# A gated feature map in two passes: 16 rows of pass two loaded between the passes instead of 16 kept rows at the end of pass one

## The chip, the cores and the metric

The kernel runs on one core of a Trainium2 chip. The metric is the device time of one execution in microseconds; the median of three runs of the kernel before is 722.75 us (721.04 to 722.99).

## The reference

```python
x: (1, 384, 384, 384) bf16, w1d: (1,) bf16
g = jnp.einsum("bhwc->bc", x) / (H * W)      # mean of each channel
s = sigmoid(g * w1d[0])                      # k = 1: one weight
return x * s[:, None, None, :]               # every pixel scaled per channel
```

The scale of each channel needs all of x, and each value of x is needed again once the scale is known. x has 113 MB, as has the result.

## The kernel before, in words

**Layout.** The 147456 pixels are 1152 "rows" on 128 partitions: a row holds one pixel of 384 channels on each partition, 768 bytes per partition and 98,304 bytes in all. SBUF holds an arena of 275 rows (line 188). The program gives it names by row number: U = 108, G0 = 116, V = 212, A = 220, T = 259, Y = 267.

**Pass one** reads all 1152 rows. SyncE issues the loads (`load`, line 231); TensorE adds each row to one accumulator in PSUM with a matmul against ones (`sum_rows`, line 253, recorded at line 242). Some of the rows are *streamed*: read, summed, overwritten. The others are *kept*, so that pass two needn't read them again. Two kinds are kept:
- Folded groups. The bf16 values of x are small enough that the upper exponent bits are known; `fold` (line 292, VectorE lines 276 and 282, ScalarE's test line 313) stores the bits of every fourth row in those spare bits of three others, so 32 rows (16 or 24 in two of the groups) take three quarters of their place. It works in a scratch of 16 rows, T and Y. Group 1 lies at rows 12 to 43, group 2 at 116 to 147, and so on in two columns.
- Raw rows, N_RAW of them: U (8 rows), V (8), the three slots of 13 rows from A on, and before the change also Y (8) and T (8), loaded when the last group is folded and the scratch is free (lines 437 and 438).

What is neither is streamed: N_STREAM = 1152 - N_RAW - 296, here 785. The order of pass one's loads is written out: group 9 (24 rows), group 0 (16 rows), then the head of the stream (lines 402 to 412), then each of the groups 1 to 8 followed by the streamed rows that `BETWEEN` gives it (361 rows in all), then the raw rows. The head has `first` = N_STREAM - 361 = 424 rows: first the remainder by 48 (40 rows) into rows 172 to 211, then loads of 48 rows that go round the slots 28 to 75, 76 to 123, 124 to 171 and 172 to 219, eight of them. Group 1 comes next, then 48 rows into 68 to 115.

**Order and waits.** `Flow` (line 21) records every instruction with the arena rows that it reads and writes and puts in the semaphore waits: a load waits until the instructions that last used its rows are done. All loads and stores of both passes go through SyncE's queue (L236 loads, L466 stores) in the order in which they were recorded; an instruction that waits holds up those behind it.

**The scale.** After the last sum ScalarE computes `s_bf` (line 443) and copies it to PSUM (line 447). VectorE then multiplies (`scale`, line 451), and SyncE stores.

**Pass two.** A planner in the program (lines 564 to 760) orders VectorE's and SyncE's work by its own costs per row: scaled pieces are stored, groups are unfolded (`unfold`, line 470) when the rows that they need for scratch are stored (`needed`, line 607), and streamed rows are loaded again into rows that have become free. `landed` is its list of pieces that are ready to scale; before, it starts with Y, U, T, V and two of the slots (lines 620 to 623). `todo` counts the streamed rows that were given out for loading.

Of the kernel before, what the change touches and what calls it, by code (L numbers as in the profile page):

```python
# [127 lines left out]
def kernel(  # L128
# [26 lines left out]
    PAIR = 2 * PIECE  # L155
    PAIRS = 4
    U = 3 * PIECE + PAIRS * 3 * PAIR
    G0 = U + PAIR
    V = G0 + PAIRS * 3 * PAIR
    A = V + PAIR  # L160
    N_A = 39
    T = A + N_A
    Y = T + 2 * PIECE
    ROWS = Y + 2 * PIECE
# [9 lines left out]
    BANKED = len(GROUPS)  # L174
    GROUPS.append((A, 6))
    PS = 3 * GROUPS[BANKED][1]
    N_RAW = ROWS - V + PAIR
    pool = ctx.enter_context(tc.tile_pool(name="sb", bufs=1))
    psum = ctx.enter_context(tc.tile_pool(name="psum", bufs=1, space=bass.MemoryType.PSUM))

# [21 lines left out]
    def view(t, r0, n):  # L202
        return t[r0 * P : (r0 + n) * P, :].rearrange("(p r) c -> p r c", r=n)

    def rows(lo, n):
        return [("a", r) for r in range(lo, lo + n)]
# [4 lines left out]

    N_STREAM = RPP - N_RAW - sum(4 * q for _, q in GROUPS)
    N_KEPT = RPP - N_STREAM
    assert N_STREAM % 2 and N_KEPT % 2
    STREAMED, KEPT = (0, N_STREAM), (N_STREAM, N_KEPT)
# [5 lines left out]
    c_raw = r  # L221
    assert r + N_RAW == N_KEPT

    def raw(a):

        return c_raw + (a - U if a < G0 else PAIR + a - V)
# [4 lines left out]
    def load(chunk, a, lo, hi):  # L231

        r0, n = chunk
        fl.add(
            "SP",
            lambda: nc.sync.dma_start(out=arena[:, a : a + hi - lo, :], in_=view(xf, r0, n)[:, lo:hi, :]),  # L236
            writes=rows(a, hi - lo), dma=True,
        )
# [150 lines left out]
    for i, bk in enumerate(banks):  # L389
        lo, hi = i * BANK, min((i + 1) * BANK, PS * C)  # L390
# [3 lines left out]
    S1, S2, S3 = ([slot] for slot in SLOTS)  # L394
# [38 lines left out]
    def take_raw(a, n):  # L433
        load(KEPT, a, raw(a), raw(a) + n)
        sum_rows(a, n)

    for a, n in S2 + [(U, 8)] + S3 + S1 + [(V, 8), (Y, 8), (T, 5), (T + 5, 3)]:
        take_raw(a, n)
    assert summed[0] == RPP

    fl.add(
        "ACT",
# [128 lines left out]
    moves, waiting, over, acts = deque(), deque(), deque(), deque()  # L571
    landed = deque()
    idle = [False] * ROWS
    todo = 0

    def release(a, n):
        for i in range(a, a + n):
# [39 lines left out]
        return f  # L617


    for a, n, end in ((Y, 4, True), (Y + 4, 4, True), (U, 4, True), (U + 4, 4, True), (T, 8, True), (V, 8, True)):  # L620
        landed.append((KEPT, a, raw(a), n, end))
    for a, n in SLOTS[:2]:
        landed.append((KEPT, a, raw(a), n, True))

# [63 lines left out]
    while True:  # L688

        if dve_at <= now:  # L690
# [4 lines left out]
            if landed and (ahead < PENDING or not can):  # L695
                chunk, a, lo, n, end = landed.popleft()
# [13 lines left out]
        if alongside and alongside[0][0] <= now:  # L710
            _, chunk, a, lo, n = alongside.popleft()
            store(chunk, a, lo, lo + n)
            moves.append([now + LAT, n * ROW + PER_STORE, stored(a, n)])
        while waiting and waiting[0][0] <= now:
            _, n, then, chunk, a, lo, known = waiting.popleft()
# [12 lines left out]
        if bank_at is None and len(line) <= total - BANKS_AT and got and max(got)[0] >= PS * 4 // 3:  # L728
            a = max(got)[1]
# [3 lines left out]
            for i, bk in enumerate(banks):  # L733
                lo, hi = i * BANK, min((i + 1) * BANK, PS * C)
# [4 lines left out]
        if got and todo < N_STREAM:  # L739
            n, a = max(got)  # L740
            n = min(n, CAP, N_STREAM - todo)
# [52 lines left out]
```

## Time and profile before

| what | value |
|---|---|
| median of three runs | 722.75 us |
| profiled execution, first to last instruction (span) | 719.4 us |
| VectorE busy | 493.9 us (69%) |
| TensorE busy | 213.0 us (30%) |
| ScalarE busy | 115.7 us (16%) |
| bytes moved | 303.79 MB, 422 GB/s over the span |
| read from HBM, written to HBM | 190.41 MB, 113.25 MB |

The page gives busy time per engine, then the span in 40 slices of 18 us in tenths of busy time. PEclk is TensorE's granted clock. In answers with windows the columns after the length are busy time and number of instructions of TensorE, its weight loads, VectorE, ScalarE and GpSimd, then granted clock, the mean busy share of the 16 DMA engines, and GB/s. In a timeline a row is start, duration, engine, line, operation and count, and in brackets the engine's idle time before it and what ended it.

### The profile page before, as it was taken

How to read it: one execution, taken by the hardware profiler on the slowest of the kernel's cores; microseconds unless marked ns; L12 is line 12 of the kernel's file. 1: busy time of each engine (PE TensorE's matmuls, PEld its weight loads, DVE VectorE, ACT ScalarE, POOL GpSimd, SP SyncE). 2: the span in 40 equal slices, each digit the busy share in tenths (PEclk: the TensorE clock that was granted, in tenths of full speed). 3: DMA queues.
4: the chain of work that ended last, by engine and by line, in shares of the span. 5: the costliest groups of instructions: out<-in, count | busy, mean ns of one | idle time of the engine just before them, and what ended most of it. 6: DMA issues, size and time to landing. Idle time of an engine off the chain costs nothing.

```text
span 719.4 us, 2061 instructions
## 1 busy us (share of the span) xinstructions
PE 213.0 (30%) x1202; PEld 0.3 (0%) x3; DVE 493.9 (69%) x471; ACT 115.7 (16%) x93; POOL 10.6 (1%) x7
## 2 busy tenths in 40 slices
PE   4677788897987770000000000000000000000000
PEld 0000000000000000000000000000000000000000
DVE  4600004788999719988999998999998985095500
ACT  3600003566677610002000000000000000000000
POOL 0000000000000005000000000000000000000000
PEclk9899999999999995555555555555555555555555
DMA  9999999999999979999999999999999999999997
GB/s 379 435 433 435 426 428 435 438 434 425 426 426 429 427 326 376 421 391 423 430 430 437 430 428 441 428 433 435 430 436 433 429 437 428 441 432 427 440 439 314
DMA packets 20174, 303.79 MB, mean 422 GB/s; under 512 B 2243, under 2 KB 2243, under 8 KB 6083
## 3 DMA queue, kind: packets, MB, share of 16 engines
q1 hardware_dynamic: 20160, 303.67, 99.0%
q8 instruction: 4, 0.07, 0.0%
q14 instruction: 8, 0.06, 0.0%
q10 hardware_dynamic: 2, 0.00, 0.0%
HBM read 190.41 MB, written 113.25 MB: 422 GB/s over the span
## 4 chain that ended last, share of the span: by engine, by line
DMA 63%; DVE 23%; PE 6%; ACT 2%; another core or an unknown queue 1%; SPq 1%; issue 0%; DVEq 0%
DMA arena<-in_x_dram 42%; DMA out_dram<-arena 20%; DVE arena L456 16%; PE bank L242 6%; DVE arena L276 4%; DVE arena L282 3%; ACT arena L313 2%; SPq L236 1%; ACT s_bf L443 0%; SPq L789 0%; DVEq L112 0%; SPq L106 0%
## 5 line engine op out<-in xcount | busy, mean ns | idle before, releaser
L456 DVE TENSOR_TENSOR arena<-arena,s_bf 128x4608 bf16<-128x4608 bf16 (+8 forms) x97 | 228.7, 2390 | 68.2 <-DMA arena<-in_x_dram 52.2
L276 DVE TENSOR_SCALAR arena<-arena 128x1536 uint16<-128x1536 uint16 (+2 forms) x247 | 145.3, 633 | 111.6 <-DMA arena<-in_x_dram 101.8
L242 PE MATMUL bank<-arena,ones 128*128 128x384 bf16 x1151 | 204.6, 339 | 46.3 <-DMA arena<-in_x_dram 46.3
L313 ACT ACTIVATE arena<-arena 128x3072 uint16<-128x3072 uint16 (+1 forms) x38 | 102.4, 2696 | 142.1 <-DVE arena L276 142.1
L282 DVE TENSOR_TENSOR arena<-arena 128x1536 uint16<-128x1536 uint16 (+2 forms) x114 | 121.0, 1061 | 5.2 <-PE bank L242 2.8
L529 PE MATMUL bank<-odd,ones 128*128 128x1 bf16 x1 | 0.2, 187 | 322.6 <-DVE odd L524 322.6
L456 POOL TENSOR_TENSOR arena<-arena,s_bf 128x1536 bf16<-128x1536 bf16 (+1 forms) x3 | 10.4, 3481 | 268.7 <-ACT bank L447 268.7
L386 ACT COPY arena<-bank 128x512 uint32<-128x512 uint32 (+1 forms) x7 | 4.0, 570 | 58.2 <-DMA out_dram<-arena 58.1
L456 DVE TENSOR_TENSOR arena<-arena,bank 128x1536 bf16<-128x1536 bf16 (+2 forms) x7 | 11.3, 1689 | 0.0
L242 PE MATMUL bank<-zeros,ones 128*128 128x384 bf16 x48 | 8.3, 326 | 0.0
L313 ACT ACTIVATION_READ_ACCUMULATOR arena<-arena 128x1 f32 x38 | 7.1, 186 | 0.0
L386 ACT COPY bank<-arena 128x512 uint32<-128x512 uint32 (+1 forms) x7 | 3.6, 567 | 0.0
L443 ACT ACTIVATE s_bf<-bank,w_sc 128x384 bf16<-128x384 f32 x1 | 0.6, 580 | 14.5 <-PE bank L242 14.5
L256 PE MATMUL bank<-arena,ones 128*128 128x384 bf16 x1 | 0.5, 480 | 6.8 <-DMA arena<-in_x_dram 6.8
L762 ACT ACT_TABLE_LOAD x1 | 1.3, 1283 | 0.7 <-PEq L778 0.7
L343 DVE TENSOR_SCALAR w_sc<-bank 128x1 f32<-128x1 f32 x1 | 0.2, 157 | 1.2 <-PE bank L338 1.2
L333 DVE MEMSET ones<- 128x128 bf16 x1 | 0.2, 165 | 1.0 <-SPq L106 1.0
L338 PE MATMUL bank<-w_bf,ones 1*128 1x1 bf16 x1 | 0.2, 179 | 2.2 <-DMA w_bf<-in_w1d_dram 2.2
L529 PEld LDWEIGHTS bank<-odd,ones 128*128 128x128 bf16 x1 | 0.1, 105 | 581.5 <-DVE odd L524 581.5
L533 DVE CAST odd_i<-bank 128x1 int32<-128x1 f32 x1 | 0.2, 157 | 0.3 <-PE bank L529 0.3
L447 ACT COPY bank<-s_bf 128x192 uint32<-128x192 uint32 x1 | 0.3, 322 | 0.0
L519 DVE TENSOR_REDUCE worst<-seen 128x1 f32<-128x38 f32 x1 | 0.2, 186 | 0.0
(8 smaller groups left out, 0.9 us busy)
## 6 DMA issues: line engine op xcount, KB each, us to landing
arena<-in_x_dram SPq DMA_DIRECT2D x15, 4608.0 KB, 34.8
arena<-in_x_dram SPq DMA_DIRECT2D x21, 1248.0 KB, 13.5
out_dram<-arena SPq DMA_DIRECT2D x7, 3072.0 KB, 33.1
arena<-in_x_dram SPq DMA_DIRECT2D x6, 3072.0 KB, 27.5
out_dram<-arena SPq DMA_DIRECT2D x4, 4608.0 KB, 39.3
arena<-in_x_dram SPq DMA_DIRECT2D x6, 2304.0 KB, 18.5
arena<-in_x_dram SPq DMA_DIRECT2D x3, 4512.0 KB, 27.1
out_dram<-arena SPq DMA_DIRECT2D x10, 1248.0 KB, 11.9
```

The source lines that it names most:

```text
L236: lambda: nc.sync.dma_start(out=arena[:, a : a + hi - lo, :], in_=view(xf, r0, n)[:, lo:hi, :]),
L242: return pe.add_instruction(mybir.InstMatmult(name=nc.get_next_instruction_name(), ins=[pe.lower_ap(rhs), pe.lower_ap(ones[:])], outs=[pe. ...
L256: return nc.tensor.matmul(acc, lhsT=ones[:], rhs=arena[:, i, :], start=first, stop=last)
L276: lambda: nc.vector.tensor_scalar(out=dst, in0=src, scalar1=s0, scalar2=s1, op0=op0, op1=op1),
L282: "DVE", lambda: nc.vector.tensor_tensor(out=dst, in0=a, in1=b, op=op), reads=reads, writes=writes
L313: lambda: nc.scalar.activation(out=y, in_=y, func=ACTF.Copy, accum_out=seen[:, 2 * k + i : 2 * k + i + 1]),
L386: "ACT", lambda: nc.scalar.copy(dst.bitcast(u32), src.bitcast(u32)), reads=reads, writes=writes
L443: lambda: nc.scalar.activation(out=s_bf[:], in_=acc, func=ACTF.Sigmoid, scale=w_sc[:, 0:1]),
L447: "ACT", lambda: nc.scalar.copy(s_ps.bitcast(u32), s_bf[:].bitcast(u32)), reads=["s_bf"], writes=["bank0"]
L456: lambda: vec.tensor_tensor(out=v, in0=v, in1=s[:, None, :].to_broadcast([P, n, C]), op=Op.mult),
L529: lambda: nc.tensor.matmul(votes, lhsT=ones[:], rhs=odd[:], start=True, stop=True),
L762: nc.scalar.preload_act_table(ACTF.Sigmoid)
```

## The change

The rows Y and T are no longer kept. N_RAW falls from 71 to 55, and N_STREAM rises from 785 to 801, so that the head of pass one has 440 rows: 8, and nine loads of 48. The raw rows now end with V, cut into 5 and 3. Behind the last load of pass one, and ahead of the scale in the program, stand two loads of 8 rows each, the first 16 rows of the stream, into Y and T; they are not summed there, but in their turn at the head of pass one. The planner starts with `todo` = 16, and with U (2, 2 and 4 rows) and V (4 and 4) ahead of Y and T.

```diff
-    N_RAW = ROWS - V + PAIR
+    N_RAW = T - V + PAIR
+    N_AHEAD = ROWS - T
...
-    for a, n in S2 + [(U, 8)] + S3 + S1 + [(V, 8), (Y, 8), (T, 5), (T + 5, 3)]:
+    for a, n in S2 + [(U, 8)] + S3 + S1 + [(V, 5), (V + 5, 3)]:
         take_raw(a, n)
     assert summed[0] == RPP
+
+
+    for a, lo in ((Y, 0), (T, PAIR)):
+        load(STREAMED, a, lo, lo + PAIR)
+    assert N_AHEAD == 2 * PAIR
...
-    todo = 0
+    todo = N_AHEAD
...
-    for a, n, end in ((Y, 4, True), (Y + 4, 4, True), (U, 4, True), (U + 4, 4, True), (T, 8, True), (V, 8, True)):
-        landed.append((KEPT, a, raw(a), n, end))
+    for a, n in ((U, 2), (U + 2, 2), (U + 4, 4), (V, 4), (V + 4, 4)):
+        landed.append((KEPT, a, raw(a), n, True))
+    for a, lo in ((Y, 0), (T, PAIR)):
+        landed.append((STREAMED, a, lo, PAIR, True))
```

## The prediction

> **What bounds the kernel now.** I read the page first: the span, the 40 slices, then the chain of waits that ended last.
>
> ```profile
> span 719.4 us, 2061 instructions
> ...
> PE   4677788897987770000000000000000000000000
> ...
> DMA  9999999999999979999999999999999999999997
> GB/s 379 435 433 435 426 428 435 438 434 425 426 426 429 427 326 376 421 391 423 430 430 437 430 428 441 428 433 435 430 436 433 429 437 428 441 432 427 440 439 314
> ```
>
> The DMA row is 9 in all slices but the one where pass one turns into pass two and the last one. Moving bytes sets the time, in both passes; any time in which the DMA engines have nothing queued is added to the end. The span is 719.4 us and the median of the runs 722.75, so 3.4 us lie around it; I add my sum to both.
>
> Next, the hand-over between the passes, in windows of 2 us, and one window fitted to the hole.
>
> ```profile
> 264.00:266.00 2.00, 1.83 (x13) 0.00 (x0) 0.00 (x0) 0.00 (x0) 0.00 (x0) 1.00 0.75 302
> 266.00:268.00 2.00, 2.00 (x13) 0.00 (x0) 0.00 (x0) 0.00 (x0) 0.00 (x0) 1.00 0.09 36
> 268.00:270.00 2.00, 0.09 (x1) 0.00 (x0) 1.26 (x2) 0.90 (x2) 0.86 (x1) 1.00 0.00 0
> 270.00:272.00 2.00, 0.00 (x0) 0.00 (x0) 2.00 (x3) 0.00 (x0) 2.00 (x1) 1.00 0.73 295
> ...
> 266.84:270.58 3.74, 1.25 (x8) 0.00 (x0) 1.84 (x3) 0.90 (x2) 1.44 (x1) 1.00 0.00 0
> ```
>
> The last two columns are the DMA share and GB/s. Most engines run out near 265, the last one at 266.84, and nothing moves until 270.58: 3.74 us of idle on the last engine. That hole is what the change means to use.
>
> Then I asked in which order pass one's loads may be issued, for the change alters that list too: SyncE's waits, the chain inside pass one, and TensorE's timeline there.
>
> ```profile
> SPq L236 <- PE bank L242: 168.0, 23, 26.8
> ```
>
> ```profile
> 88.16 8.28 PE bank L242 x40
> 96.44 0.02 issue
> 96.45 31.90 DMA arena<-in_x_dram
> ```
>
> ```profile
> 43.61 9.64 PE L242 MATMUL bank<-arena,ones 128*128 128x384 bf16 x48 [2.91 <-DMA arena<-in_x_dram]
> 55.55 7.96 PE L242 MATMUL bank<-arena,ones 128*128 128x384 bf16 x48 [2.30 <-DMA arena<-in_x_dram]
> 66.42 9.64 PE L242 MATMUL bank<-arena,ones 128*128 128x384 bf16 x48 [2.91 <-DMA arena<-in_x_dram]
> 77.29 7.96 PE L242 MATMUL bank<-arena,ones 128*128 128x384 bf16 x48 [1.22 <-DMA arena<-in_x_dram]
> 88.16 9.56 PE L242 MATMUL bank<-arena,ones 128*128 128x384 bf16 x48 [2.91 <-DMA arena<-in_x_dram]
> ...
> 109.92 0.32 PE L242 MATMUL bank<-arena,ones 128*128 128x384 bf16 x1 [2.94 <-DMA arena<-in_x_dram]
> ```
>
> A load waits until TensorE has summed the rows that it overwrites (168 us of such waits), but each wait ends while two or three loads of 48 rows are still queued. The load issued at 96.45 takes 31.90 us to land: it stands in a long queue, and so the waits cost nothing.
>
> **Part 1: the hand-over, 16 rows more in a hole.** Pass one reads 1152 rows either way. Pass two reads 801 rows instead of 785, so 16 rows (128 x 16 x 768 bytes, 1.573 MB) are moved in addition; the window 112 to 262 ran at 429 GB/s, which makes 3.7 us. They go into the hole: Y and T are free once the folding is done, at 253.5 in the trace (ScalarE's last test ends at 253.45), long before the DMA queue reaches them, so the two loads follow pass one's last bytes without a gap and end where pass one's bytes end now, in the same place of the queue. What remains of the hole: TensorE's last rows are now V, not T. All in today's times: the row "261.59 3.57 x21" sums the slot before V and V and ends at 265.16; from the last sum to VectorE's first scale were 0.65 us (268.09 to 268.74); a scale of 2 rows I estimate at 0.5 from the rows of 4 (0.96) and 13 (2.76); from the store's issue to its first packet were 0.85 (269.73 to 270.58). The first store moves at 267.2, the last engine is free at 266.84: 0.4 us are left of 3.74. Saved 3.3; the 16 rows, which pass one now reads ahead of this point, push all of it back by 3.7: **+0.4 us**. The bounds are 0 (the sums keep up with the bytes) and +3.7 (the first stores come no earlier). Everything after that is the same work: 1152 rows stored, 785 loaded. One scale more on VectorE (about 0.1 us) lies beside the stores, which it feeds at 0.22 us a row against 0.23 us of DMA; without that cover it costs its 0.1.
>
> **Part 2: the order of pass one's loads, which the change shifts without saying so.** N_STREAM rises from 785 to 801. The loads that stand between the groups are fixed (361 rows), so the head of pass one gets 440 rows instead of 424: 8 + 9 x 48 instead of 40 + 8 x 48. The 48-row loads go round four slots (28 to 75, 76 to 123, 124 to 171, 172 to 219). Before, the eighth ends in the slot 172 to 219. After, the ninth goes to 28 to 75. The next load in SyncE's queue is group 1, rows 12 to 43, and it overlaps 28 to 43. Before, that slot was written four loads back: the group's load was issued at 80.08, after 16 matmuls of the batch that began at 77.29, with 144 rows (33 us) queued behind. After, it must wait until the load **just ahead of it** has landed and 16 of its rows are summed, with nothing queued behind. SyncE issues in order, so all later loads stand behind this wait. The DMA engines run dry, and pass one has no slack elsewhere to give it back.
>
> The price: from the last packet to the landing 0.28 (266.84 to the landing event at 267.12); from the landing to the issue 2.83 as the trace has it now (77.25 to 80.08, TensorE at granted clock 1.00), or more at half clock; then 0.85 to the first packet (1.01 for the kernel's first load, 0.96 to 1.97). At full clock that is 4.0. At half clock: from 88.12 to 92.5 TensorE did 17 matmuls at granted clock 0.62, and in the batch at 66.42 the sixteenth ended near 70.4; so 16 matmuls take 4.0 to 4.3 and the hole is 5.1 to 5.5. Which one? Four batches began after an idle time of 2.9 us, and three of them show half clock and 9.6 us; the slow batches come in turn with fast ones, and by that turn the ninth load falls on a slow one. I take 4.1: **0.28 + 4.1 + 0.85 = 5.2 us**. The mean engine ends 1.7 us before the last one (at 265 against 266.84 at the hand-over), so seen from it the hole is up to 7; both ends, 4.0 and 7, go into the range.
>
> [...]
>
> Is there a second hole? The load after group 1 (rows 68 to 115) waits for all 48 rows of the same ninth load: 8.0 to 9.7 us after its landing, plus 0.9; group 1's 32 rows keep the engines busy until 3.7 + 7.3 = 11.0 (full clock) or 5.0 + 7.3 = 12.3 (half). Covered by 1.3 us or more. The two loads behind that wait for nothing new, and from group 1's landing on, loads, sums and folding stand to each other as now: the queue is 112 to 128 rows deep again two loads later.
>
> **Part 3: pass two's plan.** The planner starts from other pieces and sends U and V first, Y and T last, and all later loads are cut anew. Reading SyncE's queue with the rows that stand behind each awaited store, the thinnest cover is 21 rows now and 21 after; at the end, the last load still has 36, 16, 16, 16 and 8 rows of stores behind it, and VectorE's 3.4 us for 16 rows stay under the DMA's 3.7. I cost this at nothing. The unknown: the front of pass two moves fewer bytes, with the engines counted busy:
>
> ```profile
> 272.00:290.00 18.00, 0.00 (x0) 0.00 (x0) 17.97 (x15) 0.00 (x0) 7.52 (x3) 0.51 1.02 396
> 290.00:320.00 30.00, 0.00 (x0) 0.00 (x0) 27.28 (x27) 0.00 (x0) 0.00 (x0) 0.50 1.00 402
> 320.00:700.00 380.00, 0.19 (x1) 0.10 (x1) 306.92 (x236) 3.99 (x7) 0.00 (x0) 0.50 1.01 433
> ```
>
> Against 433 the first two windows lose 1.5 and 2.1 us, together 3.7; most of it in 280 to 284 (326 GB/s) and 312 to 316 (274). Whether another order has this too, the trace can't say: between -3.7 and +3.7, taken at 0, since the pieces there stay as small.
>
> **Sum:** 0.4 + 5.2 + 0 = +5.6 us: span 725.0, time 722.75 + 5.6 = **728.3 us**. Its own range: 4.0 to 7 for the hole, 0 to 1 for the hand-over, 726.7 to 730.8.
>
> **Rivals.**
> - *The hole is short or partly paid back*: full clock (4.0), the sums keep up (0), part of the slow front doesn't return (up to -2.4): 724.3 to 726.7. For it: the batch at 109.92, after 2.94 us idle, ran at full speed. Chance 0.18.
> - *No hole*: the load of group 1 finds rows queued behind, as the waits of now do, and only the hand-over counts: 722.75 + 0.4 = 723.2. Against it: the row numbers above leave nothing behind it. Chance 0.05.
> - *Faster*: the order of pass two's front decides. Before, stores and loads alternate from 278.7 on; after, all kept rows are stored first and four loads follow in a row. If the alternation makes the slow front, it is won back: -3.7. It decides only where the hole is under 1.1 us (0.4 + 1.1 - 3.7 = -2.2); with no hole the time is 719.5. Against it: loads and stores alternate later too, at 433. Chance 0.03.
> - *The change doesn't do what it says*: the 16 rows are not hidden, since stores start no earlier than they would behind them or lose as much to them: +3.7 instead of +0.4, 731.6; with a long hole up to 733. Against it: 253.5 lies 13 us ahead of the hand-over. Chance 0.09.
>
> The forecast has 0.65. The range leaves out the two small cases, the lower end of the first rival and the upper end of the last: 725.2 to 731.2. Within 0.3% (720.6 to 724.9, about what a measurement of this kernel can tell from no change) fall the case without a hole and the lower end of the short one: 0.10. Faster 0.03, slower 0.87.
>
> **What would show it.** In the changed profile: a window of some 4 us near 110 to 120 with the DMA share near 0, with SyncE waiting for TensorE, and TensorE idle some 5 us more behind the ninth 48-row load (right: part 2; absent: wrong). No window of 2 us at 0 at the hand-over, and pass two's first store about 5.5 us later than 270.58 (part 1). From there to the end the same length within 2.5 us (part 3). A faster kernel, or a slower one without that hole, makes the prediction wrong.

## The result and the profile after

The changed kernel takes 730.31 us (median of 4 runs, 728.17 to 730.75) against 722.5 (721.04 to 722.99): ratio 1.0108, 95% interval 1.0096 to 1.0121, so 7.8 us slower. The profiled execution is the one of 728.17 us with a span of 726.4, so 1.8 us lie around its span; the span of 719.4 before then very likely belongs to the run of 721.04, with 1.6 us around it, and not to the median. Span against span the change costs 7.0 us.

The page of the changed kernel, the lines that answer to those of before:

```profile
span 726.4 us, 2070 instructions
...
PE   5686776988897771000000000000000000000000
...
DMA  9999996999999998999999999999999999999997
GB/s 378 434 421 449 428 424 286 434 433 434 422 425 427 428 426 366 389 428 428 427 426 429 436 424 442 425 431 436 433 434 441 433 423 446 427 428 442 424 431 320
```

The 7 at the hand-over (326 and 376 GB/s in two slices) has become an 8 (366 and 389). But the seventh slice, in the middle of pass one, has fallen from 435 to 286 GB/s. In windows of 2 us around it, with the DMA share and GB/s at the end of each line, and one window fitted to the silence:

```profile
108.00:110.00 2.00, 2.00 (x14) 0.00 (x0) 0.00 (x0) 0.00 (x0) 0.00 (x0) 1.00 0.80 340
110.00:112.00 2.00, 2.00 (x14) 0.00 (x0) 0.00 (x0) 0.00 (x0) 0.00 (x0) 1.00 0.74 313
112.00:114.00 2.00, 0.77 (x6) 0.00 (x0) 0.00 (x0) 0.00 (x0) 0.00 (x0) 1.00 0.05 18
114.00:116.00 2.00, 2.00 (x13) 0.00 (x0) 0.00 (x0) 0.00 (x0) 0.00 (x0) 1.00 0.00 0
116.00:118.00 2.00, 2.00 (x15) 0.00 (x0) 0.00 (x0) 0.00 (x0) 0.00 (x0) 1.00 0.54 135
118.00:120.00 2.00, 2.00 (x14) 0.00 (x0) 0.00 (x0) 0.00 (x0) 0.00 (x0) 1.00 0.66 270
...
113.55:117.67 4.12, 3.75 (x24) 0.00 (x0) 0.00 (x0) 0.00 (x0) 0.00 (x0) 1.00 0.00 0
```

The hole stands at its forecast place, with a slope on each side: the engines don't stop together (a share of 0.80, 0.74 and 0.05 from 108 to 114), and they don't start at full rate (270 GB/s in 118 to 120). TensorE and SyncE there, in two timelines of the changed kernel:

```profile
103.05 9.64 PE L243 MATMUL bank<-arena,ones 128*128 128x384 bf16 x48 [2.91 <-DMA arena<-in_x_dram]
113.92 7.96 PE L243 MATMUL bank<-arena,ones 128*128 128x384 bf16 x48 [1.23 <-DMA arena<-in_x_dram]
126.49 7.69 PE L243 MATMUL bank<-arena,ones 128*128 128x384 bf16 x32 [4.60 <-DMA arena<-in_x_dram]
```

```profile
116.71 0.33 SPq L237 DMA_DIRECT2D arena<-in_x_dram  x1
```

The ninth load lands at 113.88, its sums begin at 113.92, and the load of group 1 goes out at 116.71: 2.83 us after the landing, as it did before, but now with nothing queued behind it.

### The profile page after: what moved, and what is told of

It is laid out like the page before. It is cut to its first block, busy times and chain, and to the rows that moved or that the text cites. A ratio compares the mean times of both kernels' runs of the same rounds, so it can differ in the third digit from the quotient of the medians.

```text
span 726.4 us, 2070 instructions
## 1 busy us (share of the span) xinstructions
PE 213.4 (29%) x1202; PEld 0.3 (0%) x3; DVE 494.0 (68%) x473; ACT 115.7 (16%) x93; POOL 10.2 (1%) x7
## 4 chain that ended last, share of the span: by engine, by line
DMA 62%; DVE 22%; PE 8%; another core or an unknown queue 5%; ACT 1%; issue 0%; SPq 0%
DMA arena<-in_x_dram 48%; DVE arena L462 15%; DMA out_dram<-arena 14%; PE bank L243 8%; DVE arena L277 4%; DVE arena L283 3%; ACT arena L314 1%; SPq L237 0%; ACT s_bf L449 0%; SPq L472 0%; SPq L797 0%; SPq L112 0%; SPq L106 0%
## 5 line engine op out<-in xcount | busy, mean ns | idle before, releaser
L462 DVE TENSOR_TENSOR arena<-arena,s_bf 128x4608 bf16<-128x4608 bf16 (+9 forms) x98 | 228.4, 2363 | 91.6 <-DMA arena<-in_x_dram 78.6
L462 DVE TENSOR_TENSOR arena<-arena,bank 128x1536 bf16<-128x1536 bf16 (+3 forms) x8 | 11.8, 1544 | 0.0
```

The source lines that it names most:

```text
L462: lambda: vec.tensor_tensor(out=v, in0=v, in1=s[:, None, :].to_broadcast([P, n, C]), op=Op.mult),
```

## Where the 7 us are: lost bytes, stage by stage

The DMA engines move 433 GB/s in the middle of pass two of the kernel before (320 to 700; 431 in the changed one), and I take 433 as the full rate for both. So the time that a stretch loses is its length times (433 - its GB/s) / 433. Three stretches, before (first fence) and after (second), the later ones shifted with the first store:

```profile
90.00:150.00 60.00, 52.37 (x305) 0.00 (x0) 27.02 (x37) 20.05 (x15) 0.00 (x0) 0.96 1.00 433
...
258.00:274.00 16.00, 8.61 (x50) 0.00 (x0) 5.26 (x6) 0.90 (x2) 4.86 (x2) 0.95 0.70 288
274.00:326.00 52.00, 0.00 (x0) 0.00 (x0) 49.25 (x42) 0.00 (x0) 5.52 (x2) 0.50 1.01 402
```

```profile
90.00:150.00 60.00, 48.38 (x269) 0.00 (x0) 19.09 (x26) 14.28 (x10) 0.00 (x0) 0.91 0.91 388
...
265.00:281.00 16.00, 8.78 (x53) 0.00 (x0) 4.60 (x6) 0.90 (x2) 4.20 (x2) 0.91 0.87 359
281.00:333.00 52.00, 0.00 (x0) 0.00 (x0) 49.72 (x42) 0.00 (x0) 5.77 (x2) 0.50 1.01 413
```

| stretch | lost before | lost after | difference |
|---|---|---|---|
| ahead of group 1 (60 us) | 0.0 | 6.2 | +6.2 |
| hand-over (16 us) | 5.4 | 2.7 | -2.7 |
| 16 rows more, 1.573 MB at 433 GB/s | | 3.6 | +3.6 |
| front of pass two (52 us) | 3.7 | 2.4 | -1.3 |

The sum is +5.8 of the 7.0. The first row depends on the edges of its window by up to 1 us: 100 to 140, at 355 GB/s, gives 7.2. The landings of later loads need no window and give 6.6 (below the table of the four holes). What then remains, 0.8, is spread out, most of it over the long rest of pass two (431 GB/s from 333 to 720, 432 before from 326 to 713).

## The experiments

The theory on trial: the order of pass one's loads makes nearly all of the loss, and the change itself (16 rows more, hidden in the hand-over) is about even. The rivals: the additional rows and pass two's new plan cost; or pass one pays the hole back.

**1. The changed kernel with the slots turned,** so that the ninth load ends where the eighth did.

```diff
-    EARLY = [(A - 48 * i, 48) for i in (4, 3, 2, 1)]
+    EARLY = [(A - 48 * i, 48) for i in (1, 4, 3, 2)]
```

> The changed kernel, with one edit: the nine 48-row loads at the head of pass one start at the slot 172 to 219, so that the ninth ends there again, as the eighth did before, and the load of group 1 waits for rows that were loaded four loads back. Theory (the hole ahead of group 1 is nearly the whole cost): the hole is gone, DMA share 0.9 or more in all windows of 2 us from 100 to 130, and the time is that of the kernel before plus the 0.4 us of the hand-over: 722.5 to 723.5. Rival (the 16 additional rows and pass two's new order cost): it stays at 728 or more.

722.11 us against 721.89, ratio 1.0004 (0.9995 to 1.0013). Three windows of it, the last two for the hand-over and the front of pass two:

```profile
90.00:150.00 60.00, 49.76 (x292) 0.00 (x0) 24.82 (x34) 18.83 (x13) 0.00 (x0) 0.97 1.00 432
258.00:274.00 16.00, 9.23 (x55) 0.00 (x0) 4.16 (x6) 0.90 (x2) 3.76 (x2) 0.94 0.88 364
274.00:326.00 52.00, 0.00 (x0) 0.00 (x0) 49.93 (x42) 0.00 (x0) 6.21 (x2) 0.50 1.01 415
```

The hole is gone and with it the whole loss. What the change says of itself costs nothing that can be measured, and wins nothing. The expected share of 0.9 in every window of 2 us was asked too sharply: packets count where they start, so that such windows swing (0.77 in 100 to 102, 1.24 in the next), and the kernel before swings as much (0.68 in 124 to 126). The time lies below the expected 722.5 to 723.5 because the kernel before ran at 721.89 here, and not at 722.5.

**2. The hole alone, in the kernel before.** Nothing of the change is in it; the eight loads start one slot later.

```diff
-    EARLY = [(A - 48 * i, 48) for i in (4, 3, 2, 1)]
+    EARLY = [(A - 48 * i, 48) for i in (3, 2, 1, 4)]
```

> The kernel before, with one edit: the eight 48-row loads start one slot later, so that the eighth ends in 28 to 75 and group 1's load must wait for it; nothing of the change itself is in. Theory, by lost bytes (the windows 108 to 122 of the changed kernel move 3.06 MB less than at 434 GB/s, that is 7.0 us): 722.5 + 7.0 = 729.5. Second theory, by the last DMA engine's idle time alone (4.0 us between its packets): 726.5. Rival (the hole is paid back later in pass one, and pass two costs): 722.5.

729.12 against 721.89, ratio 1.0097 (1.0081 to 1.0112): +7.2 us, as the first theory has it (its 3.06 MB are 3.11 by the windows of 2 us of the trace, that is 7.2 us and not 7.0). Together with the first experiment this settles the cause from both sides. Here TensorE ran the sums that group 1's load waits for at half clock (the batch at 109.97 took 9.43 us, granted clock 0.50 up to 113, and the load went out at 114.22, 4.30 after the landing at 109.92). The hole is longer for it:

```profile
90.00:150.00 60.00, 50.52 (x274) 0.00 (x0) 21.13 (x29) 15.89 (x11) 0.00 (x0) 0.89 0.89 379
109.58:115.17 5.59, 5.20 (x24) 0.00 (x0) 0.00 (x0) 0.00 (x0) 0.00 (x0) 0.70 0.01 3
```

No data packet moves for 5.6 us (the 3 GB/s are one packet of the instruction queue, q8, at 111.03), but 60 x (433 - 379) / 433 = 7.5 us of bytes are lost.

**3. The ninth load in two pieces,** 20 and 28 rows in the same slot.

```diff
-    stream_all(EARLY, first - first % 48)
+    stream_all(EARLY, first - first % 48 - 48)
+    stream_all([(A - 192, 20), (A - 172, 28)])
```

> The changed kernel, with the ninth 48-row load cut into 20 rows (28 to 47) and 28 rows (48 to 75) in the same slot. Group 1's load still waits for the load just ahead to land and 16 of its rows to be summed, but 28 rows (6.4 us) are queued behind that. Theory (what costs is that nothing is queued, not the wait): no hole, since landing, sums and first packet take 4.0 us; 722.5 to 723.5, as with the slots turned. Rival (the wait itself, or the slot order, costs): 728 or more.

724.97, ratio 1.0048 (1.0034 to 1.0062): +3.1 us, a miss of the expectation, though far from the rival's 728. The timeline shows what the expectation left out:

```profile
103.22 15.96 PE L243 MATMUL bank<-arena,ones 128*128 128x384 bf16 x96 [2.92 <-DMA arena<-in_x_dram]
```

The piece of 20 rows lands at 107.73, but TensorE is still summing the load ahead of it and comes to these rows only near 111; group 1's load goes out at 113.81, when the 28 rows behind are all but read.

```profile
90.00:150.00 60.00, 50.60 (x292) 0.00 (x0) 22.06 (x30) 16.86 (x11) 0.00 (x0) 0.94 0.96 410
113.96:114.76 0.80, 0.76 (x5) 0.00 (x0) 0.00 (x0) 0.00 (x0) 0.00 (x0) 1.00 0.00 0
```

The miss teaches more than a hit would have: all engines are silent for 0.8 us only, yet 3.2 us of bytes are lost, and the time is 3.1 longer. The silence of the last engine is not the price of a hole.

**4. A sum sooner, in the tail** (the first experiment, with U loaded after the two last slots).

```diff
-    for a, n in S2 + [(U, 8)] + S3 + S1 + [(V, 5), (V + 5, 3)]:
+    for a, n in S2 + S3 + S1 + [(U, 8), (V, 5), (V + 5, 3)]:
```

> The first experiment (slots turned), and in addition U's 8 raw rows are loaded after the last two slots of 13 instead of between them, so that TensorE has 8 rows and not 13 ahead of V's 8. Now the last sum ends 1.7 us after the last landing of pass one; by the rows (13 x 0.17 + 8 x 0.17 from the landing of the 13 rows on) it should end 1.1 us earlier, and so should the first store. Theory (after 16 rows the hand-over still has about 2 us of idle engines, 2.1 in the mean engine's measure): 0.8 to 1.2 us faster than the first experiment, 721.5 to 722.5. Rival (the loads of Y and T fill what is left for the slowest engine, so that stores come no earlier): same as the first experiment within 0.3 us.

722.71, ratio 1.0011 (1.0002 to 1.002): not faster than the first experiment. But it doesn't test what it was made for: TensorE now had 29 rows in one stretch from 264.14 on, ended at 269.01, and the first store went out at 270.25 against 270.43. The edit moved the backlog instead of shortening it. Inconclusive for the two theories; experiment 8 does it properly.

**5. The rows not loaded ahead** (the first experiment without the two loads between the passes; all 801 streamed rows are loaded in pass two).

```diff
-    for a, lo in ((Y, 0), (T, PAIR)):
-        load(STREAMED, a, lo, lo + PAIR)
...
-    todo = N_AHEAD
+    todo = 0
...
-    needed = [set(SCRATCH + rows(U, 8)), set(SCRATCH + rows(V, 8)), set(SCRATCH)]
+    needed = [set(rows(U, 8)), set(rows(V, 8)), set()]
...
-    for a, lo in ((Y, 0), (T, PAIR)):
-        landed.append((STREAMED, a, lo, PAIR, True))
...
+    unused = True
...
+        if unused and now >= 6.0:
+            release(T, 8)
+            unused = False
```

> The first experiment (slots turned), without the two loads between the passes: Y and T stay empty at the hand-over, T's 8 rows are given out for loading 6 us into the plan of pass two, Y is scratch from the start; all 801 streamed rows are loaded in pass two. It has the change's additional bytes, but none of them in the hand-over. Theory (the loads fill idle time of the DMA engines at the hand-over: 5.2 us lost in the kernel before, 2.4 in the first experiment): 2.8 us slower than the first experiment, 724.5 to 725.5. Rival (the hand-over is not where the 16 rows are hidden; pass two has room for them): 722 to 723.

725.54 against 721.76, ratio 1.0048 (1.0033 to 1.0063), 3.4 us above the first experiment by the medians and 3.2 by the ratios. The hand-over and the front of pass two:

```profile
258.00:274.00 16.00, 9.42 (x55) 0.00 (x0) 3.88 (x6) 0.90 (x2) 3.48 (x2) 0.97 0.63 260
274.00:326.00 52.00, 0.00 (x0) 0.00 (x0) 50.04 (x42) 1.07 (x2) 6.48 (x2) 0.50 1.01 417
```

The hand-over loses 6.4 us here and 2.5 in the first experiment (364 GB/s in the same window, shown there). So the loads do hide in idle time, and hiding is worth what the 16 rows cost (3.6): the change buys the rows their own price back, no more.

**6. A longer hole** (the second experiment, with the eighth load's rows summed from the last to the first, so that group 1's load waits for 48 sums).

```diff
-        for i in range(a, a + n):
+        for i in (range(a + n - 1, a - 1, -1) if back else range(a, a + n)):
...
-    stream_all(EARLY, first - first % 48)
+    stream_all(EARLY, first - first % 48 - 48)
+    stream(48, A - 192, back=True)
```

> The second experiment (the kernel before, the eighth load in 28 to 75), with the rows of that eighth load summed from the last to the first, so that group 1's load waits for all 48 sums and not for 16. From landing to issue it takes 8.0 us at full clock or 9.6 at half, against 4.3 measured in the second experiment. Theory (each microsecond of the hole goes to the end): 729.1 + 3.8 to 5.4 = 732.9 to 734.5. Rival (later stages of pass one pay part of it back): under 731.

733.82 against 721.76, ratio 1.0176 (1.0157 to 1.0194), +12.1 us. The sums ran at full clock, 8.0 us from the landing at 109.69 to the issue at 117.72.

```profile
90.00:150.00 60.00, 44.20 (x251) 0.00 (x0) 18.19 (x24) 13.93 (x9) 0.00 (x0) 0.89 0.83 351
109.34:118.67 9.33, 7.96 (x48) 0.00 (x0) 0.00 (x0) 0.00 (x0) 0.00 (x0) 1.00 0.02 4
```

Nothing is paid back that the noise would let one see. The four holes side by side:

| kernel | all engines silent | bytes lost, 60 us | later loads land later by | time against before |
|---|---|---|---|---|
| 3, ninth load in two | 0.8 | 3.2 | 3.2 | +3.1 |
| the change | 4.1 | 6.2 | 6.6 | +7.8 |
| 2, hole alone | 5.6 | 7.5 | 8.0 | +7.2 |
| 6, longer hole | 9.3 | 11.4 | 11.8 | +12.1 |

Silence plus 1.9 to 2.4 us makes the lost bytes, and the lost bytes make the time within 1.6 us (the intervals of the ratios reach 0.9 to 1.4 us to each side). The fourth column needs no window: it takes the time from one landing ahead of the hole (in the change the last 48-row load but one, 103.01) to the landing of the fifth load behind group 1 (175.20), with the same rows between them in all kernels, and compares with the kernel before (98.98 and 164.59). By it each hole costs its silence and 2.4 to 2.5 us; with the slots turned (experiment 1) 0.3 us are left.

**7. The kernel before, sooner** (last slot loaded as 7 and 6 rows, Y scaled first as 2, 2, 4).

```diff
-    for a, n in S2 + [(U, 8)] + S3 + S1 + [(V, 8), (Y, 8), (T, 5), (T + 5, 3)]:
+    for a, n in S2 + [(U, 8)] + S3 + [(A, 7), (A + 7, 6), (V, 8), (Y, 8), (T, 5), (T + 5, 3)]:
...
-    for a, n, end in ((Y, 4, True), (Y + 4, 4, True), (U, 4, True), ...
+    for a, n, end in ((Y, 2, True), (Y + 2, 2, True), (Y + 4, 4, True), (U, 4, True), ...
```

> The kernel before, with the last slot of 13 raw rows loaded as 7 and 6, and Y scaled and stored first as 2, 2 and 4 rows instead of 4 and 4. TensorE comes to its last 16 rows with less behind it (0.44 us by the rows: last landing 267.12, three sums and the pipe 0.53, against 268.09), and the first store goes out 0.4 us sooner. Theory (with nothing loaded ahead all of the hand-over's latency is idle time of the engines, so what is cut from it is won): 0.8 us faster than the kernel before, 721.1. Rival (the first small stores lose as much, or VectorE limits the front of pass two): no difference within 0.3 us.

721.12 against 721.76, ratio 0.9987 (0.9978 to 0.9995): 0.6 us faster of 0.8 expected. The first store went out at 269.43 instead of 269.73; the sums ended no sooner (TensorE's last row ends at 268.19), so what was to be won by TensorE wasn't, and the 0.3 us by which the store went out sooner come from the smaller first piece. Where the other 0.3 us lie wasn't tried, and the interval (0.4 to 1.6 us) holds both sizes. The gain needs none of the change.

**8. The first experiment, sooner** (last slot loaded as 7 and 6 rows).

```diff
-    for a, n in S2 + [(U, 8)] + S3 + S1 + [(V, 5), (V + 5, 3)]:
+    for a, n in S2 + [(U, 8)] + S3 + [(A, 7), (A + 7, 6), (V, 5), (V + 5, 3)]:
```

> The first experiment (slots turned), with the last slot of 13 raw rows loaded as 7 and 6. TensorE's last sum should end about 1.0 us earlier (last landing 267.47 and 0.68, against 269.19). Theory (the mean engine still has 2.1 us idle at the hand-over): up to 1.0 us faster than the first experiment, 721.1. Rival (the slowest engine is through with the loads ahead 0.4 us before the first store reaches it, and sets when pass two starts): 0.4 us at most, 721.7 to 722.4.

720.85 against 721.76, ratio 0.9984 (0.9974 to 0.9993): the fastest of all, 1.3 us below the first experiment by the medians and 1.4 by the ratios, with some 0.9 us of uncertainty. The sums end at 268.31 instead of 269.19, and the first store goes out at 269.55 instead of 270.43. In the profiled executions the hand-over loses 1.8 us (384 GB/s in 258 to 274) against 2.5, but the front gives this back (409 against 415 GB/s), and the spans are 719.7 and 719.5. The medians speak for the theory of the mean engine; one profile of each doesn't show where all of it went, and I leave that open. Against experiment 7 the difference (0.3 us) is smaller than the intervals.

## Why the prediction was right, point by point

- **The hole (part 2): place and mechanism right, size too small.** It said 0.28 + 4.1 + 0.85 = 5.2 us. The two errors had opposite signs. The sums ran at full clock (1.00 granted from 114 to 118), 2.83 and not 4.1; the idle time ahead of the ninth batch was 1.23 us, where I had reckoned with 2.9. With that my sum would have been 4.0, and the engines' common silence is 4.1. But the silence is not the price. The engines end some 2 us apart and start again below full rate (270 GB/s in 118 to 120), and 6.2 us of bytes were lost, 6.6 by the landings. With the bytes of each packet of the trace spread over its duration, 1.5 us go in the slope ahead of the silence and 0.9 behind it. So the term that was mis-sized is the hole, 5.2 for 6.2 to 6.6; that it came so near is in part luck, since 1.3 us too much for the clock stood against 2.4 left out for the slopes. The prediction had this, seen from the mean engine, as its upper end of 7 (its 1.7 us, from 265 and 266.84, are 1.8), and its value should have lain near that end. Of the second hole that I ruled out there is no trace: group 1 (load issued 116.71) is followed at 121.91 by the next load, ahead of the end of its bytes.
- **The hand-over (part 1): +0.4 forecast, +0.9 measured** (3.6 us of bytes, 2.7 saved, not 3.3). The shape was right: sums behind the bytes, the first store 1.23 us after the last sum, and 0.4 us idle on the last engine (277.39 to 277.83). But here too the last engine was the wrong measure; the mean engine still loses 2.5 to 2.7. Without the hole, in experiment 1, the first store's packets start at 271.28, 0.7 us later than the 270.58 of before.
- **Pass two (part 3): 0 forecast, -1.3 at its front.** Its cause wasn't tried. The front loses 2.4, 2.2, 2.3, 1.9 and 2.9 us with the changed plan (the change and experiments 1, 4, 5 and 8), and 3.7 and 3.4 with the plan of before (the kernel before and experiment 7), so the rival that wanted 3.7 from it had a third of its size, and no chance against the hole. The gain doesn't reach the end either: from the first store's packets on it is 448.6 us (277.83 to 726.4) against 448.8 before.
- **The base.** I took 3.4 us around the span, the distance of the fastest run's span from the median; around one run it is 1.6 to 1.8. This shifts where the forecast starts from, not the sum: +5.6 forecast, +7.8 measured by the medians and +7.0 by the spans.
- **The signs that it named.** The silence stood at 113.55 to 117.67, with SyncE's next load waiting for the sums, and TensorE was idle for 4.60 us behind them. At the hand-over no window of 2 us fell to 0 (the lowest has 75 GB/s, 276 to 278). The first store came 7.3 us later, not 5.5, and the rest took as long as before.
- **Rivals.** "No hole" and "the change doesn't do what it says" are ruled out by experiments 1, 2 and 5. "The hole is short": its first half happened (full clock), its conclusion did not.
- **The half clock.** In the changed kernel, batches after 2.9 us of idle time took 7.96, 7.96, 7.96 and 9.64 us, those after 4.3 and 5.4 us took 9.6; in experiment 2 one after 2.94 took 9.43. So neither "three of four" nor the turn of slow and fast held, and the length of the gap alone didn't settle the clock. Between 16 and 255 us the traces of the two kernels show half clock eleven times, nine times for 3.41 us and twice for 6.83. Windows of 3.41 us in the changed kernel, around a gap behind which the clock stayed full and one behind which it was half:

```profile
86.88:90.29 3.41, 2.40 (x15) 0.00 (x0) 0.00 (x0) 0.00 (x0) 0.00 (x0) 1.00 1.10 476
90.29:93.70 3.41, 1.52 (x10) 0.00 (x0) 0.00 (x0) 0.00 (x0) 0.00 (x0) 1.00 0.90 389
...
100.53:103.95 3.42, 0.90 (x6) 0.00 (x0) 0.00 (x0) 0.00 (x0) 0.00 (x0) 1.00 1.12 485
103.95:107.36 3.41, 3.41 (x13) 0.00 (x0) 0.00 (x0) 0.00 (x0) 0.00 (x0) 0.50 0.88 378
```

In the 3.41 us ahead of each of the eleven, matmuls took 0.00 to 1.33 us; ahead of the stretches that stayed at full clock, windows cut in the same step have 1.48 us or more. That is what these two traces show; what sets the clock was not tried.

## What to carry to other kernels

A change of one count can turn a rotation of buffers: work out, for each load, which earlier load last used its place and how many bytes stand queued behind that one; here a load whose place was the one just filled found nothing queued behind that one, and no data moved for 4.1 us in the changed kernel and 5.6 in experiment 2. Price such a hole by lost bytes (length times missing rate) or by how much later the loads behind it land, not by the silence of all engines, which fell short of it by 1.9 to 2.5 us in the four holes. And the rows moved into idle time at this hand-over won what they cost, no more (3.4 us by experiment 5, for 3.6 us of bytes); if the same rows could have been kept, the hand-over itself must get shorter before anything is won.

## What the runs showed of the hardware that was not expected

In this stream of loads, a queue that ran dry cost about 2.4 us beyond its silence: in four holes of 0.8 to 9.3 us the lost bytes were 1.9 to 2.4 us, and the delay of later landings 2.4 to 2.5 us, more than the time in which no data moved. At the load ahead of the hole the first engine's part landed at 111.97 and the last one's at 113.88. After the restart the engines stood close together (125.80 and 126.44 for group 1), but two loads later they were 1.3 us apart again and by the fifth 2.1 (173.13 and 175.20), so the closer start was gone, and nothing of the hole was paid back by it. TensorE's clock, too, went otherwise than the prediction had it: in the changed kernel four batches came after 2.9 us of idle time, and one of them ran at half clock for 3.41 us (it took 9.64 us, against 7.96 for the other three).
